# Transposing k before q for the first head pair of a top-k attention and squared-ReLU kernel, with new order tables

## The chip, the cores and the metric

The kernel runs on one NeuronCore of a Trainium2 chip. The core has five instruction streams: TensorE (PE: matrix products, transposes), VectorE (DVE), ScalarE (ACT), GpSimd (POOL) and SyncE (SP, which only issues DMAs). They run side by side and meet at semaphores. The metric is device time in microseconds (us) of one launch; lower is better.

## The reference

For 8 batches, 8 heads, 576 positions and a head width of 64, each row of scores keeps its 32 largest entries; the result of the attention feeds a two-layer network with a squared ReLU.

```python
def _attn_ref(q, k, v):
    scores = scale * np.matmul(q, k.transpose(0, 1, 3, 2))
    kth = np.partition(scores, -top_k, axis=-1)[..., -top_k:-top_k + 1]
    scores = np.where(scores >= kth, scores, -1000000000.0)
    attn = np.exp(scores - np.max(scores, axis=-1, keepdims=True))
    attn = attn / (np.sum(attn, axis=-1, keepdims=True) + 1e-09)
    return np.matmul(attn, v)

def _moe_ref(x, w_in, w_out):        # x: 4608 x 512, d_ff = 2048
    r = np.maximum(x @ w_in, 0.0)
    return (r * r) @ w_out
```

## The kernel before

**Units.** The heads are taken in pairs, 32 pairs in all. A unit is a block of 128 queries of one pair (or two 64-query ends of two pairs); there are 144, numbered here from 0. For each unit PE makes the scores of both heads into a slot of PSUM (the pool `large` has two slots), ACT copies them to the tile `s` (L1053), and DVE and POOL find the 32nd largest value of each row: DVE folds the score columns by maxima (L1131), lists the largest eight again and again (L1178, L1193, L1173) and ends with `kth` (L1196, once for each head); POOL does two integer passes between (L1126). ACT turns `s` and `kth` into the mask `w` (L1219, once for each head), PE transposes `s` and adds the mask to it in PSUM (the products `ident,s` and `steep_bf,w`), ACT takes the exponential `p` (L1285), PE multiplies by v, and so on. When all heads of a block of rows are done, PE runs the network on it (`xt,win`, then `wo,g`), with ReLU on ACT (L1443) and squares on POOL (L1458) or ACT.

**Order.** Every operation is declared with `pl.op(engine, ...)`: `r` names tiles that it reads (it then waits for all operations that write them), `hold` a tile that it merely occupies, `after` operations to wait for, `order` operations that it must only be issued behind. `arrange` doesn't schedule: the table `ORDER` lists for each engine the operations in the order in which they are issued, and `SLOT` lists the slot of each tile. In `ORDER["pe"]` small numbers are warm-up products of `ones_bf` by itself, 128x512, which write a PSUM bank that nothing reads, and a negative number is a spare: three products of `ident_bf` into an idle part of a score tile. Both only keep TensorE at work.

**The first pair.** `load_first` (L892) loads it by seven DMAs (L904): k's rows 0 to 511 of head 0 and the last 64 rows of both heads on ACT's queue, and on SP's queue k's rows 0 to 511 of head 1, q's first 128 rows of both heads (tile `rq`), and the rest of q (tile `rq2`). The two DMAs on ACT's queue are one operation with one semaphore, `d_rk0`; the one on SP's queue has `d_first`. `first_pair` (L917) then transposes on PE: `o_x` turns q's first 128 rows, `o_k` the four main blocks of k, and a third one the last 64 rows of k. `o_k` is bound behind `o_x` and reads `rk`, so it waits for all three loads of k. DVE copies k's main rows to the tile `qk` (L934), ACT the other two parts (L933, L935), and unit 0's scores can start. From the second pair on `load_pair` (L947) does the same in six DMAs on SP's queue (L955, L956), with the copies on ACT (L1006 to L1008).

**The end.** `verdict` (L1691) checks on DVE, from kept maxima, whether a fast way of finding the 32nd value was valid, and sets a flag; if it was not, the whole is done again by a slower way (which the profiled execution doesn't enter). Its operations (L1703 to L1733) stand among the last units' in DVE's order.

Of the kernel before, what the change touches and what calls it, by code (L numbers as in the profile page):

```python
# [663 lines left out]
def bass_top_k_attn__then__act_relu_squared_kernel(  # L664
# [219 lines left out]
    def build(full, weights, pl):  # L884
# [7 lines left out]
        def load_first(b, hp, rq, rq2, rk, base):  # L892
# [10 lines left out]
            def start(queue, *parts):  # L903
# [8 lines left out]
                  sem=slot_sem, ndma=1)  # L912
            pl.op("sp", 3.5, base - 79, start(
                nc.sync, lambda: part(rq2, q, 0, 1, 3), lambda: part(rq2, q, 1, 1, 3), lambda: rest(rq2, q, 512, 0)),
                w=[rq2], take=[rq2], sem=slot_sem, ndma=3)

        def first_pair(rq, rq2, rk, rv, qk, vb, base):  # L917
            tk, tx, tq = Tile(psum), Tile(psum), Tile(psum)
# [816 lines left out]
    main = Plan()  # L1735
# [108 lines left out]
```

## Time and profile before

| what | value |
|---|---|
| median of 3 runs | 745.13 us (744.3 to 746.08) |
| the profiled execution's own time | 746.16 us |
| its span, first to last instruction | 744.3 us |
| granted TensorE clock, mean | 0.995 of 2.4 GHz |
| busy: DVE, ACT, PE, POOL | 719.4, 717.3, 706.4, 685.9 us |
| PE products: warm-up of `ones_bf`, spares of `ident_bf` | 56, 138 |

The profiled execution's span is 1.86 us below its own time, and its own time is 1.03 us above the median. Four engines are busy for over 90% of the span, so what one engine loses is not made up elsewhere unless that engine has idle time later. "Busy" counts the stretch in which at least one instruction of the engine is under way. The row of an instruction says how long the engine was idle before it and which instruction ended the idle time.

### The profile page before, as it was taken

The numbers are of one execution on the slowest core, as the hardware profiler recorded it, in microseconds if no ns is written. First come the engines' busy times: TensorE is split into PE (matmuls) and PEld (weight loads), VectorE is DVE, ScalarE is ACT, GpSimd is POOL, SyncE is SP. The second block draws the span as 40 slices with busy tenths as digits, with TensorE's granted clock in tenths as the row PEclk, the third lists the DMA queues.
The fourth block names the chain that finished last, engine by engine and source line by source line (L and its number), as shares of the span: only waits on it lengthen the run. The fifth ranks groups of instructions, "written<-read, shape, count | busy, mean of one in ns | idle before, by whom it ended". The sixth has DMA issues, their size and how long they took to land.

```text
span 744.3 us, 27788 instructions
## 1 busy us (share of the span) xinstructions
PE 706.4 (95%) x10712; PEld 530.0 (71%) x10712; DVE 719.4 (97%) x3397; ACT 717.3 (96%) x1276; POOL 685.9 (92%) x529
## 2 busy tenths in 40 slices
PE   8898899999999999989999999999999999999997
PEld 4565777767677676767778677777777777777876
DVE  5999999999999999999999999999999999999996
ACT  4899999999999999999999999999999999999984
POOL 3799999999999999999999999999999999999971
PEclk9999999999999999999999999999999999999999
DMA  9766544254342432134311733121643115211101
GB/s 181 165 170 175 134 102 73 70 87 78 67 84 48 84 79 52 44 70 85 82 35 36 125 92 64 27 48 56 117 75 80 28 44 93 58 35 32 37 16 51
DMA packets 172730, 57.31 MB, mean 77 GB/s; under 512 B 157744, under 2 KB 164912, under 8 KB 172592
## 3 DMA queue, kind: packets, MB, share of 16 engines
q1 hardware_dynamic: 164528, 51.19, 30.2%
q0 software_dynamic: 7392, 4.13, 4.7%
q8 instruction: 85, 1.39, 0.8%
q14 instruction: 53, 0.43, 0.2%
q10 hardware_dynamic: 672, 0.16, 0.1%
HBM read 40.83 MB, written 13.57 MB: 73 GB/s over the span
## 4 chain that ended last, share of the span: by engine, by line
ACT 59%; PE 21%; DVE 16%; issue 3%; ACTq 0%
PE ps L875 17%; ACT w L1219 16%; ACT p L1285 12%; ACT s L1053 12%; ACT g L1443 6%; ACT s L1183 5%; DVE s L1131 4%; PE ps L878 4%; DVE s L1193 3%; DVE c L1178 3%; ACT av L1388 2%; DVE kth L1196 2%; DVE s L1173 2%; ACT o L1479 2%; ACT g L1461 1%
## 5 line engine op out<-in xcount | busy, mean ns | idle before, releaser
L1126 POOL TENSOR_TENSOR u<-s 128x864 int32<-128x864 int32 x142 | 244.7, 1723 | 22.1 <-DVE s L1131 20.8
L1219 ACT ACTIVATE w<-s,kth 128x576 bf16<-128x576 f32 x286 | 245.9, 918 | 2.9 <-DVE kth L1196 2.8
L1126 POOL TENSOR_TENSOR s<-s,u 128x864 int32<-128x864 int32 x142 | 243.1, 1714 | 3.2
L1178 DVE MAX8 c<-s 128x8 f32<-128x106 f32 (+2 forms) x864 | 203.3, 264 | 0.0
L1131 DVE TENSOR_TENSOR s<-ps,s 128x288 f32<-128x288 f32 x432 | 192.2, 445 | 9.9 <-ACT s L1053 7.7
L875 PE MATMUL ps<-qk 64*128 64x192 f32 (+3 forms) x1280 | 179.5, 430 | 8.5 <-DVE s L1131 4.6
L1053 ACT COPY s<-ps 128x1152 f32<-128x1152 f32 (+1 forms) x145 | 180.2, 1244 | 4.8 <-PE ps L875 4.1
L1285 ACT ACTIVATE p<-ps 128x1152 bf16<-128x1152 f32 x143 | 180.9, 1265 | 1.7 <-PE ps L875 1.5
L1193 DVE MATCH_REPLACE8 s<-c,s 128x92 f32<-128x92 f32 (+2 forms) x716 | 179.5, 254 | 0.0
L875 PEld LDWEIGHTS ps<-qk 64*128 64x128 f32 (+1 forms) x1280 | 130.8, 176 | 39.3 <-DVE s L1131 11.4
L875 PE MATMUL ps<-wo,g 128*128 128x512 bf16 (+1 forms) x592 | 144.5, 374 | 0.8 <-ACT qk L1007 0.4
L875 PE MATMUL ps<-xt,win 128*128 128x256 bf16 (+1 forms) x1280 | 130.7, 252 | 1.7 <-ACT g L1443 0.9
L1196 DVE MAX8 kth<-s 128x8 f32<-128x296 f32 x288 | 127.9, 454 | 0.3 <-POOL s L1186 0.2
L1173 DVE MAX8 s<-s 128x8 f32<-128x288 f32 x288 | 125.3, 446 | 0.3 <-POOL s L1126 0.2
L878 PEld LDWEIGHTS ps<-ident,s 64*128 64x128 f32 x2592 | 97.0, 139 | 35.9 <-ACT w L1219 13.5
L878 PE MATMUL ps<-ident,s 64*128 64x64 f32 x2592 | 112.4, 228 | 8.8 <-ACT w L1219 7.1
L875 PEld LDWEIGHTS ps<-xt,win 128*128 128x128 bf16 x1280 | 99.0, 98 | 21.0 <-issue 4.0
L1443 ACT ACTIVATE g<-ps 128x512 bf16<-128x512 f32 x140 | 98.2, 745 | 0.2
L1458 POOL TENSOR_TENSOR g<-g 128x1024 bf16<-128x1024 bf16 x50 | 94.6, 1892 | 3.8 <-ACT g L1443 3.7
L875 PEld LDWEIGHTS ps<-wo,g 128*128 128x128 bf16 x592 | 50.2, 98 | 48.1 <-issue 4.3
L1183 ACT ACTIVATE s<-s,c 128x140 f32<-128x140 f32 x148 | 76.4, 558 | 0.0
L875 PEld LDWEIGHTS ps<-vb,p 128*128 128x128 bf16 (+1 forms) x1600 | 54.6, 101 | 22.7 <-ACT p L1285 4.5
(92 smaller groups left out, 779.0 us busy)
## 6 DMA issues: line engine op xcount, KB each, us to landing
out_dram<-o SPq DMA_DIRECT2D x32, 256.0 KB, 2.8
rk<-in_k_dram SPq DMA_DIRECT2D x63, 128.0 KB, 2.6
rq<-in_q_dram SPq DMA_DIRECT2D x62, 128.0 KB, 2.6
s<-s SPq DMA_DIRECT2D x144, 32.0 KB, 1.9
g<-in_moe_w_in_dram SPq DMA_DIRECT2D x8, 512.0 KB, 4.4
g<-in_moe_w_out_dram SPq DMA_DIRECT2D x8, 512.0 KB, 4.1
vd<-in_v_dram POOLq DMA_DIRECT2D x14, 288.0 KB, 4.5
vb<-vd SPq DMA_DIRECT2D x56, 64.0 KB, 2.3
```

What stands on the lines that cost most here:

```text
L875: return pe.matmul(o, l, r, start=start, stop=stop, skip_group_check=True)
L878: return pe.matmul(o, i, ident, is_transpose=True, skip_group_check=True, **kw)
L1053: return pl.op("act", .14 + 2 * (c1 - c0) / 1200, pl.at("copy", tg - LEAD + 1), lambda: act.copy(at(st)[:, :, c0:c1], two(banks(ss)[:, FIR ...
L1126: return pl.op("gp", dur, prio, lambda: gp.tensor_tensor(o().bitcast(I32), x().bitcast(I32), y().bitcast(I32), op), **kw)
L1131: return dve(.36, lambda: vec.tensor_tensor(o(), two(banks(ss)[:, FIRST_AT + c:], SECOND, QUART), x(), ALU.max), r=[ss], **kw)
L1173: prev[i] = [dve(.0685 + HALF / 960, lambda i=i: vec.max(area(LIST, LIST + 8, i), area(LESS, LESS + HALF, i)), after=prev[i] + [low], hold ...
L1178: lambda i=i, t=t, span_=span_: vec.max(eighth(t, i), span_(i)),
L1193: lambda i=i, t=t, span_=span_: vec.match_replace(span_(i), eighth(t, i), span_(i), NEG), hold=[st])]
L1196: ks.append(chain(kth, i, prev[i], .0685 + (8 + HALF) / 960, lambda i=i: vec.max(eighth(kth, i), area(BIGS - QUART, LIST + 8, i)), hold=[st]))
L1219: masks[i:] = [pl.op("act", .77, pl.at("mask", tw + .8 * i), lambda i=i: act.activation(at(wt)[:, i, :], at(st)[:, i, 0:S], ACTF.Relu, bia ...
L1285: return act.activation(at(pt)[:, :, :].rearrange("p c (h q) -> p h c q", h=2), bass.AP(x.tensor, x.offset, [x.ap[0], [APART, 2], [64, 9], ...
L1443: return act.activation(at(g)[:, g0:g0 + 512], bank(hh)[:, 0:512], ACTF.Relu)
```

## The change

The four DMAs keep their queues and their order. The two on ACT's queue become two operations: the main rows (`main`, with the load on SP's queue), and the last 64 rows (`edge`) with a semaphore of their own. In `first_pair` the order of the transposes is turned: `o_k` comes first and waits for `main` alone, `o_x` follows, then k's last 64 rows, which wait for `edge`. The planned durations of these operations are new numbers; they only feed the bookkeeping of `arrange`. The tables `ORDER` and `SLOT` are new as a whole. By count, each engine issues the same instructions as before, except that PE has 49 warm-up products instead of 56 and 105 spares instead of 138. In the block ahead of the first transposes there are 6 warm-up products instead of 9, and ahead of the second pair's there are 2 instead of 5.

```diff
     "pe": (
-        "90 91 92 93 94 95 96 97 98 2541 2542 2543 2547 2574 2579 101 100 104 106 102 2613 2614 2615 2620 2648 -4979 -4979 -4979 -4979 -4979 126 119 129 134 "
+        "136 94 188 91 222 100 2542 2543 2544 2548 2575 2580 148 244 2614 2615 2616 -4979 -4979 -4979 2621 -4979 -4979 2649 2687 2689 2688 2694 2578 2757 "
...
-            pl.op("sp", .1, base - 82, start(nc.scalar, lambda: part(rk, k, 0, 0, 4),
-                                             lambda: rest(rk, k, 512, 0)),
-                  w=[rk], take=[rk], sem=slot_sem, ndma=2, via="act")
-            pl.op("sp", 4.0, base - 81, start(nc.sync, lambda: part(rk, k, 1, 0, 4)), w=[rk], sem=lambda o: "first", ndma=1)
-            pl.op("sp", 3.5, base - 80, start(nc.sync, lambda: (at(rq)[:, 0, :, :], both)), w=[rq], take=[rq],
+            main = [pl.op("sp", 3.3, base - 82, start(nc.scalar, lambda: part(rk, k, 0, 0, 4)),
+                          w=[rk], take=[rk], sem=slot_sem, ndma=1, via="act")]
+            edge = pl.op("sp", 4.2, base - 81.9, start(nc.scalar, lambda: rest(rk, k, 512, 0)), w=[rk], sem=lambda o: "edge",
+                         ndma=1, via="act")
+            main.append(pl.op("sp", 2.5, base - 81, start(nc.sync, lambda: part(rk, k, 1, 0, 4)), w=[rk],
+                              sem=lambda o: "first", ndma=1))
+            pl.op("sp", 2.65, base - 80, start(nc.sync, lambda: (at(rq)[:, 0, :, :], both)), w=[rq], take=[rq],
                   sem=slot_sem, ndma=1)
-            pl.op("sp", 3.5, base - 79, start(
+            pl.op("sp", 2.1, base - 79, start(
                 nc.sync, lambda: part(rq2, q, 0, 1, 3), lambda: part(rq2, q, 1, 1, 3), lambda: rest(rq2, q, 512, 0)),
                 w=[rq2], take=[rq2], sem=slot_sem, ndma=3)
+            return main, edge
...
-            o_x = pl.op("pe", .15, base - 45.2, flips(tx, rq, [0]), r=[rq], w=[tx], take=[tx, qk])
-            o_k = pl.op("pe", .5, base - 45.1, flips(tk, rk, [0, 1, 2, 3]), r=[rk], w=[tk], take=[tk], order=[o_x])
+            o_k = pl.op("pe", 1.03, base - 45.2, flips(tk, rk, [0, 1, 2, 3]), hold=[rk], w=[tk], take=[tk, qk], after=main)
+            o_x = pl.op("pe", .27, base - 45.1, flips(tx, rq, [0]), r=[rq], w=[tx], take=[tx], order=[o_k])
             pl.op("pe", .2, base - 45, lambda: tr(bank(tx)[:, 128:192], at(rk)[0:64, 4, :, :].rearrange("p h d -> p (h d)"),
-                                                  ident32[0:64, 0:64]), r=[rk], w=[tx], order=[o_k])
+                                                  ident32[0:64, 0:64]), hold=[rk], w=[tx], after=[edge], order=[o_x])
```

**PE from its start to the first scores.** Before (`ones_bf` is a warm-up product, `ident,rq` and `ident,rk` transposes of q and k, `qk` the scores; what stands behind "waits" are semaphores):

```order
L875 MATMUL ps<-ones_bf 128x512 [waits s_dve]
L875 MATMUL ps<-ones_bf 128x512
L875 MATMUL ps<-ones_bf 128x512 [waits s_pe] x7
L878 MATMUL ps<-ident,rq 128x128 [waits s_gp,d_rq0,s_pe]
L878 MATMUL ps<-ident,rk 128x128 [waits d_first,d_rk0]
L878 MATMUL ps<-ident,rk 128x128 x3
L878 MATMUL ps<-ident,rk 128x64
L875 MATMUL ps<-qk 128x192 [waits s_dve,s_act]
```

In the change (its line numbers are lower by one on PE, higher by two behind `load_first`):

```order
L874 MATMUL ps<-ones_bf 128x512 [waits s_dve]
L874 MATMUL ps<-ones_bf 128x512
L874 MATMUL ps<-ones_bf 128x512 [waits s_pe] x3
L874 MATMUL ps<-ones_bf 128x512
L877 MATMUL ps<-ident,rk 128x128 [waits d_first,d_rk0,s_gp,s_pe]
L877 MATMUL ps<-ident,rk 128x128 x3
L877 MATMUL ps<-ident,rq 128x128 [waits d_rq0,s_pe]
L877 MATMUL ps<-ident,rk 128x64 [waits d_edge]
L874 MATMUL ps<-qk 128x192 [waits s_dve,s_act]
```

Three warm-up products are gone, the four main transposes of k stand ahead of that of q, and k's last 64 rows wait for `d_edge`, which the main ones no longer wait for.

**PE at unit 4's scores (the third pair's first unit) and unit 0's masked transposes (`ident,s`, `steep_bf,w`).** Before:

```order
L878 MATMUL ps<-ident,rk 128x128 [waits s_pe]
L878 MATMUL ps<-ident,rk 128x128 x3
L875 MATMUL ps<-ident_bf 128x128 [waits s_act]
L875 MATMUL ps<-ident_bf 128x128 x2
L878 MATMUL ps<-ident,s 128x64 [waits s_act]
L878 MATMUL ps<-ident,s 128x64 x16
L878 MATMUL ps<-ident,s 128x64 [waits fence]
L875 MATMUL ps<-steep_bf,w 128x64 x17
L875 MATMUL ps<-steep_bf,w 128x64 [waits fence]
L875 MATMUL ps<-qk 128x192 [waits s_act,s_dve]
L875 MATMUL ps<-qk 128x384 x2
L875 MATMUL ps<-qk 128x192 [waits fence]
```

In the change:

```order
L877 MATMUL ps<-ident,rk 128x128 [waits s_act]
L877 MATMUL ps<-ident,rk 128x128 x3
L874 MATMUL ps<-qk 128x192 [waits s_dve,s_act]
L874 MATMUL ps<-qk 128x384 x2
L874 MATMUL ps<-qk 128x192 [waits fence]
L877 MATMUL ps<-ident,s 128x64 [waits s_dve,s_act]
L877 MATMUL ps<-ident,s 128x64 x16
L877 MATMUL ps<-ident,s 128x64 [waits fence]
L874 MATMUL ps<-steep_bf,w 128x64 x17
L874 MATMUL ps<-steep_bf,w 128x64 [waits fence]
```

The scores of unit 4 stand ahead of unit 0's masked transposes, not behind them, and the three spares between are gone.

**DVE at the last unit (L1212 and L1214 write the last unit's mask, L1703 and L1705 are operations of `verdict`).** Before:

```order
L1193 MATCH_REPLACE s<-c,s 128x2x70 [waits s_dve]
L1178 MAX c<-s 128x8 [waits s_dve]
L1196 MAX kth<-s 128x8 [waits s_dve]
L1193 MATCH_REPLACE s<-c,s 128x2x70 [waits s_dve]
L1196 MAX kth<-s 128x8 [waits s_dve]
L1703 TENSOR_TENSOR signs<-signs,c 128x2x67
L1212 TENSOR_SCALAR w<-s,kth 128x512 [waits d_d3,s_pe,s_dve]
L1395 RECIPROCAL rzall<-av 128x4 [waits s_act]
```

In the change:

```order
L1180 MAX c<-s 128x8 [waits s_dve]
L1195 MATCH_REPLACE s<-c,s 128x2x70 [waits s_dve]
L1397 RECIPROCAL rzall<-av 128x4 [waits s_act]
L1198 MAX kth<-s 128x8 [waits s_dve]
L1214 TENSOR_SCALAR w<-s,kth 128x512 [waits s_dve]
L1705 TENSOR_TENSOR c<-c 128x2x67
L1397 RECIPROCAL rzall<-av 128x2 [waits s_act]
L1705 TENSOR_TENSOR c<-c 128x2x67
```

The `verdict` operation that stood ahead of the last mask now comes behind it. The same holds for the one over `c`, which before stood 46 rows further up and is here the row behind the mask.

## Rows read from the trace of the kernel before

**Rows 1.** Busy time by stages: stretch, us, busy PE, PEld, DVE, ACT, POOL (instructions), clock, DMA.

```profile
0.00:30.00 30.00, 24.77 (x186) 14.95 (x188) 20.45 (x89) 16.56 (x24) 14.18 (x43) 0.94 0.89 177
30.00:627.00 597.00, 569.54 (x8652) 427.20 (x8644) 589.97 (x2801) 595.92 (x1065) 576.53 (x417) 1.00 0.37 79
627.00:741.00 114.00, 112.09 (x1890) 87.90 (x1888) 108.86 (x511) 104.84 (x189) 95.24 (x70) 1.00 0.17 38
```

**Rows 2.** Timeline, 0 to 9 us: start, duration, engine, instruction, idle before.

```profile
0.75 0.47 SPq L904 DMA_DIRECT2D rk<-in_k_dram  x1
0.76 1.25 ACTq L904 DMA_DIRECT2D rk<-in_k_dram  x2
...
1.07 4.02 PE L875 MATMUL ps<-ones_bf 128*128 128x512 bf16 x9 [1.07 <-DVE ones_bf L1622]
1.28 2.34 SPq L904 DMA_DIRECT2D rq<-in_q_dram  x4
...
5.15 0.47 PE L878 MATMUL ps<-ident,rq 128*128 128x128 f32 x1
...
5.42 1.16 PE L878 MATMUL ps<-ident,rk 128*128 128x128 f32 x5
...
6.42 0.69 DVE L934 COPY qk<-ps 128x512 f32<-128x512 f32 x1 [5.40 <-PE ps L878]
...
7.25 1.24 PE L875 MATMUL ps<-qk 64*128 64x192 f32 x8 [0.67 <-DVE qk L934]
...
8.96 1.44 DVE L1131 TENSOR_TENSOR s<-ps,s 128x288 f32<-128x288 f32 x3 [1.85 <-ACT s L1053]
```

**Rows 3.** Line L904, issues of 0.7 to 1.0 us: issue to landing.

```profile
DMA to landing us min/median/max: 3.0/3.2/3.3
```

**Rows 4.** Line L904, all seven issues: issue to landing.

```profile
DMA to landing us min/median/max: 2.9/3.1/3.5
```

**Rows 5.** Timeline of PE, 5 to 9 us: the last product of the first nine.

```profile
4.46 0.63 PE L875 MATMUL ps<-ones_bf 128*128 128x512 bf16 x1
```

**Rows 6.** Tile rk, 0 to 12 us: weight loads, ns least, median, most.

```profile
L878 PEld LDWEIGHTS ps<-ident,rk x5: 134/230/231, 5.2 to 6.3; 128*128 128x128 f32 x4, 64*128 64x128 f32 x1
```

**Rows 7.** Tile rq, 0 to 12 us: the same.

```profile
L878 PEld LDWEIGHTS ps<-ident,rq x5: 137/142/181, 5.2 to 8.9; 128*128 128x128 f32 x4, 64*128 64x128 f32 x1
```

**Rows 8.** Timeline of ACT, 13 to 40 us.

```profile
14.42 0.27 ACT L1008 COPY qk<-ps 128x128 f32<-128x128 f32 x1
...
21.23 1.44 ACT L1219 ACTIVATE w<-s,kth 128x576 bf16<-128x576 f32 x2 [1.04 <-DVE kth L1196]
...
24.16 1.13 ACT L1285 ACTIVATE p<-ps 128x1152 bf16<-128x1152 f32 x1 [1.02 <-PE ps L875]
26.25 1.12 ACT L1053 COPY s<-ps 128x1152 f32<-128x1152 f32 x1 [0.96 <-PE ps L875]
...
31.68 1.14 ACT L1053 COPY s<-ps 128x1152 f32<-128x1152 f32 x1
```

**Rows 9.** Timeline of PE, 12 to 26 us.

```profile
13.28 0.63 PE L878 MATMUL ps<-ident,rk 128*128 128x128 f32 x4 [0.30 <-DMA rk<-in_k_dram]
...
22.73 0.91 PE L878 MATMUL ps<-ident,s 64*128 64x64 f32 x18 [1.50 <-ACT w L1219]
...
23.93 2.27 PE L875 MATMUL ps<-qk 64*128 64x192 f32 x8
```

**Rows 10.** Busy time by stages, 20 to 30 us, columns as in Rows 1.

```profile
23.00:26.50 3.50, 3.50 (x45) 2.73 (x40) 3.50 (x17) 1.52 (x3) 3.02 (x5) 0.53 0.88 254
```

**Rows 11.** Timeline of DVE, from 27 us and from 712 us.

```profile
27.40 0.46 DVE L1131 TENSOR_TENSOR s<-ps,s 128x288 f32<-128x288 f32 x1 [0.81 <-ACT s L1053]
...
712.59 1.69 DVE L1703 TENSOR_TENSOR c<-c 128x134 f32<-128x134 f32 x1
...
726.14 1.39 DVE L1703 TENSOR_TENSOR signs<-signs,c 128x134 f32<-128x134 f32 x1
```

**Rows 12.** Timeline of PE, 712 to 745 us.

```profile
719.29 0.27 PE L878 MATMUL ps<-ident_bf,x 128*128 128x128 bf16 x2 [0.38 <-POOL x L1397]
```

More of the change, by code (lines that the diff above doesn't have):

```diff
@@ L32 @@
     "pe": (
[43 rows of a table removed]
-    "act": (
[38 rows of a table removed]
-    "dve": (
[121 rows of a table removed]
[42 rows of a table added]
+    "act": (
[38 rows of a table added]
+    "dve": (
[121 rows of a table added]
 }
 SLOT = (
-    "01010101010101010010101010010100000000000000001000000000000001010000000000001000000000000000000000000000000000000000000000000000000000000100"
-    "00000000000000000000000000001000100000000000000000000000000001110100001000000001010000000000000000000000000000000000000000000000000000000000"
+    "01010101010101010111110100000101010000000000001000000000000000100000000000000000000000000000000000000000000000100001000000100000000100000000"
+    "00000000010001000000000000011001100000000001100000000000000001110100001000000000100000000000000000000000000000000000000000000000000000000000"
     "00000000000000000000000000000000000000000000000000000000000000000000000000000000000000000000000000000000000000000000000000000000000000000000"
@@ L267 @@
-    "110016121001100010100111110001200111110011010030100100400010010512000006010100000101110000000011110100001201010010130012020001213011")
+    "00000000000000000000000000000000000000000000000000000000000000000000000000000000000010100000001011001000010110102000213000010011102012040101"
+    "15001010001030031610001001011010011102013000111100120002000013111111400000511010000160012110011101100011121112030010100010111201300000104141"
+    "00400000511010000010001602020000100001051110111101120010110011201131102040000100001100200310011151110100600011000101010102121210000030011111"
@@ new lines @@
+    "41100050001116020200100010001011021030101114015000102031101001012111110013041113021214100010110410011501010600100001011110001001100110000101"
+    "10210310011120110010300101411010050002161000100000011010011211120000113111204001010000111021031001110102000501001610110001503110002120110001"
+    "00102140002011113000001013001104010205000010000110021031100116111110000000111111012000213110000104000111151010060101010001211011000001011021"
+    "03010011410511010011001200110300100001402111411120500001001011311060111001000110150410010010020011100001101200310011131010100401011502000061"
@@ new lines @@
+    "01200010010101100101102011113001010401021500100010101102113000011021011010010006111000103120101403000000111014100010011210120011000310000401"
+    "01100050010060101110002001100110110011102013010011210021300101004000015101110006010210001001010000120101100011101201301001101040001210111300"
+    "10000000100115120004011110015100001060111010100000001111010010011010020000110301001001400010005010001001011001610001110000110111010010121001"
+    "00101011101301001114001011015111000160011000201000000313101141410100000000010001112010111001000111121000211100003001010004110000150011100001"
@@ L270 @@
+    "101006121011000000100011110100200110100111000130100000400011011512000006011110110011110000010111110100001201010010030012020101203011")
 class Pool:
@@ L906, in load_first, with first_pair @@
             both = bass.AP(q.tensor, q[b, 2 * hp, 0:P, :].offset, [[D, P], [S * D, 2], [1, D]])
-            pl.op("sp", .1, base - 82, start(nc.scalar, lambda: part(rk, k, 0, 0, 4),
-                                             lambda: rest(rk, k, 512, 0)),
-                  w=[rk], take=[rk], sem=slot_sem, ndma=2, via="act")
-            pl.op("sp", 4.0, base - 81, start(nc.sync, lambda: part(rk, k, 1, 0, 4)), w=[rk], sem=lambda o: "first", ndma=1)
-            pl.op("sp", 3.5, base - 80, start(nc.sync, lambda: (at(rq)[:, 0, :, :], both)), w=[rq], take=[rq],
+            main = [pl.op("sp", 3.3, base - 82, start(nc.scalar, lambda: part(rk, k, 0, 0, 4)),
[5 more added lines that the diff above has]
+            pl.op("sp", 2.65, base - 80, start(nc.sync, lambda: (at(rq)[:, 0, :, :], both)), w=[rq], take=[rq],
                   sem=slot_sem, ndma=1)
-            pl.op("sp", 3.5, base - 79, start(
+            pl.op("sp", 2.1, base - 79, start(
                 nc.sync, lambda: part(rq2, q, 0, 1, 3), lambda: part(rq2, q, 1, 1, 3), lambda: rest(rq2, q, 512, 0)),
                 w=[rq2], take=[rq2], sem=slot_sem, ndma=3)
-        def first_pair(rq, rq2, rk, rv, qk, vb, base):
+            return main, edge
+        def first_pair(rq, rq2, rk, rv, qk, vb, base, main, edge):
             tk, tx, tq = Tile(psum), Tile(psum), Tile(psum)
@@ L972, in load_pair @@
                 rq2 = tile("rq")
-                load_first(b, hp, rq, rq2, rk, base)
+                main, edge = load_first(b, hp, rq, rq2, rk, base)
             else:
@@ L985, in load_pair @@
             if via:
-                return first_pair(rq, rq2, rk, rv, qk, vb, base)
+                return first_pair(rq, rq2, rk, rv, qk, vb, base, main, edge)
             tq, tk, tx = Tile(psum), Tile(psum), Tile(psum)
```

11 lines of the change are left out of this document (removed), and 397 rows, old and new, of the table ORDER.

## Prediction

> **What bounds the kernel now.** I read the busy time by stages first. Over the first 30 us no engine but PE is busy for even 70% of the time; from 30 to 627 us ACT works for 595.92 of 597 us and DVE for 589.97; from 627 to 741 us PE works for 112.09 of 114 [rows 1]. So there are three stages: a start in which engines wait for each other, a long stage that ACT fills, and an end that PE fills. In the second stage only 1.08 us of idle time of the filling engine is left, in the third 1.91. Since each engine issues the same work as before (but for warm-up products and spares), a gain must come from the start, or out of these 3.0 us.
>
> The timeline of the start shows a chain without slack: warm-up products, six transposes, two kinds of copies, unit 0's scores at 7.25, ACT's copy, DVE's first fold at 8.96 [rows 2]. The transposes begin at 5.15, right behind the last warm-up product, which starts at 4.46 and takes 0.63 [rows 2, 5]. The DMAs had landed by then: the two main loads of k are issued at 0.75 and 0.76 and land 3.0 to 3.3 us later, so at 3.75 to 4.06 [rows 2, 3]. The last 64 rows of k are issued at about 1.3 (ACT's two issues take until 2.01) and q at 1.28; with the longest landing of all seven, 3.5, both are there by 4.8 [rows 2, 4]. What holds the first transpose is the warm-up, not a load.
>
> **The change, part by part.** *Three warm-up products fewer ahead of the transposes.* The nine start from 1.07 to 4.46, that is 0.424 apart [rows 2, 5]; the sixth starts at 3.19 and ends at 3.82. Then k's main rows are the last to come, at 4.06 at the latest. I put the first transpose at 4.1, against 5.15: 1.05 earlier.
>
> *k first, with a semaphore for its last rows.* The six transposes are the same; they took from 5.15 to 5.42 + 1.16 = 6.58, so 1.43, and unit 0's scores followed 0.67 later [rows 2]. In the new order q's turn comes some 1.2 us after 4.1 and the last rows' turn behind it, both past 4.8, so neither new wait ends later than its turn, and nothing queued behind them on PE waits longer. Had the old wait for all of k stayed, the start would have been 4.8 at the latest, so this edit is worth up to 0.7 of the 1.05 and the products the rest. Transposes end at 5.53, scores start at 6.2, the first fold at 7.9 (8.96 less 1.05). DVE's copy L934 begins 1.1 earlier too, and ends ahead of ACT's copies, which still release the scores.
>
> *Three products fewer ahead of pair 2's transposes.* Nothing: PE waits there for pair 2's k, which lands at 13.28 [rows 9]. SP issues the same DMAs in the same order over the whole start, so this landing doesn't move. Nor do unit 2's scores get earlier: ACT now copies k's last rows ahead of its main ones, which by the duration of the copies (0.27 and 0.58, the first begun at 14.2) puts them at 15.1, some 0.3 later than now. Cover: DVE has units 0 and 1 to list, and after 11.35 it has no wait of over 0.3 us until 27.40 [rows 11]. By the new order 31 of its instructions stand ahead of unit 2's first fold, some 11 us of work from 7.9 on, and the scores' copy would be there at 17.5. Without that cover the head start would be lost.
>
> *Unit 4's scores ahead of unit 0's masked transposes.* Now PE waits 1.50 for the mask, runs the masked transposes, and then makes unit 4's scores at a granted clock of 0.53 of full (mostly the level of 1.2 GHz), in 2.27 instead of 1.24 [rows 2, 9, 10]; ACT waits 0.96 for them and DVE 0.81 [rows 8, 11]. In the new order these scores wait for the third pair's copies on ACT alone: by the durations at about 22.6, copied by 25.0, or 26.0 at the half clock. DVE, with the same instructions ahead of it as now, gets there at 27.40 - 0.81 - 1.05 = 25.5, so its 0.81 goes, or shrinks to 0.5. But ACT, which fills the next stage, decides: laying out its operations by hand until it has done the same set that ends at 32.8 now [rows 8], I end at about 31.7. It loses its waits of 1.04, 1.02 and 0.96 [rows 8] only to find others of 0.6 to 0.7, for the masks come no earlier than DVE gives them. So I carry 1.05 on, and DVE's 0.8 is slack.
>
> *The rest of the tables.* From 30 to 627 us nothing in the trace before prices an unknown order. Bounds: a gain of 1.08 (all of ACT's idle time), a loss of some waits like those of the start, each near 1.0. I take 0, since ACT is full already.
>
> *The end.* Two operations of the verdict, 1.69 and 1.39 on DVE, stand ahead of the last units' lists and of the last mask [rows 11], and move behind it. But PE, which fills this stage, waits only 0.38 in one place, for POOL, itself waiting for DVE [rows 12]; what is late next is PE's own queue. Bounds: 0 and the stage's 1.91; I take 0.4, nearest to the one wait that shows.
>
> *Spares.* 33 spares and the other warm-up products less: they run where PE waits anyway, so nothing, unless the clock falls (below).
>
> Sum: -1.05 - 0.4 = -1.45. The profiled execution took 746.16, its span 744.3 and 1.86 around it, and would take 744.7. It is 1.03 above the median of the runs shown, 745.13; from the median the same sum gives **743.7**.
>
> **The rivals.** *The new order closes more gaps.* ACT's 1.08 and PE's other 1.5 are there to be had, and DVE arrives early with 0.8 of slack. Against: these gaps are many and small. All of it: 741.1; a typical share of half: 742.4.
>
> *The head start is spent.* Either at unit 2, if DVE runs out of units 0 and 1 (for: pair 2's landing is fixed), or at the clock. The weight loads of the first 128-wide transposes of k take 230 ns, later ones of q 142; the load of k's last rows, at 6.3, takes 134, as the same shape does later [rows 6, 7]. So PE ran slowly until about 6.1, although the granted clock reads full there, and unit 0's scores at 6.2 would just miss that. The new order has less work ahead of them, and a pause of 0.3 us. If the faster rate comes late, unit 0's scores take 2.27 instead of 1.24 and the 1.05 is gone: 745.13 - 0.4 = 744.7; with unit 1's too it is 745.1 or more. The Trainium skill (TensorE: Matmul & The Clock Gate, What's actually happening) says that the throttled state is the default and that activity releases it, which speaks against taking work away here. By that rule the fast rate comes later the less PE does; the trace agrees as to the slow start (230 against 142 ns), and shows no case with less work.
>
> *Slower: the clock falls more often.* With 40 products fewer, and PE waiting for masks in the first 110 us, more stretches like that of 23 to 26.5 us could come. That one cost ACT its waits of 1.02 and 0.96, 1.98 together. One more stretch makes 745.7, two make 747.6; from two on the change is slower. For: waits of PE of 1.5 us like that at 22.73 [rows 9]. Against: at unit 4 the new order puts scores into such a wait, not spares.
>
> *The change doesn't do what it says:* k's main rows land only when PE would have started anyway. They'd have to take 4.3 us instead of 3.3, and seven loads show at most 3.5 [rows 4]. Then 744.7.
>
> **How the numbers follow.** A measurement of this kernel can tell about 0.2%, 1.5 us, from no change: faster means below 743.64, slower above 746.6. The forecast, head start plus a little of the end, gets 0.45; its own range is 742.7 to 744.6, half of it below the mark (0.22 faster, 0.23 same). More gaps closed: 0.22, faster. Head start spent: 0.20, same. Clock falls: 0.10, slower. Doesn't do it: 0.03, same. That is 0.44 faster, 0.46 same, 0.10 slower. The range runs from 741.7, which leaves out the far end of the first rival, to 745.6, which leaves out the falling clock: at most 0.15 outside.
>
> **What would show it.** Right: the first `ident,rk` product at 4.1 (3.9 to 4.3), unit 0's scores at 6.2 and still 1.24 long, the first fold at 7.9, pair 2's k still landing near 13.3, no wait of DVE near 27 us, ACT full from about 29 us on. For the second rival: scores of over 1.3 us before 10 us, or a fold of unit 2 that waits. For the slower one: further stretches of granted clock near 0.5 with waits on ACT beside them. Wrong altogether: a first transpose later than 4.8, or a head start at 30 us that is gone at 627.

## Result and profile after

The changed kernel takes 749.42 us (median of 8 runs, 748.13 to 753.04) against 745.56 for the kernel before (8 runs): a ratio of 1.0055, 95% interval 1.0042 to 1.0069. It is slower by 0.55%, where 743.7 was forecast with a range up to 745.6. The profiled execution took 748.13, its span 746.3; it is the shortest of the eight, so its profile shows only about half of the loss.

The busy time by stages of the changed kernel, columns as in [rows 1]:

```profile
0.00:30.00 30.00, 21.15 (x141) 14.23 (x141) 21.02 (x91) 15.56 (x24) 14.48 (x42) 0.94 0.76 167
30.00:627.00 597.00, 566.12 (x8575) 424.27 (x8625) 587.21 (x2786) 595.43 (x1064) 575.61 (x419) 1.00 0.37 80
627.00:743.00 116.00, 109.89 (x1897) 88.55 (x1906) 109.19 (x522) 106.42 (x191) 96.29 (x70) 1.00 0.15 37
```

Against [rows 1] ACT has done 1.0 less by 30 us, and no stage looks broken (the last one is cut 2 us later, since the span ends 2 us later). So I looked for places, not for a stage. The start first, to set beside [rows 2] (timeline: start, duration, engine, instruction, idle before):

```profile
1.07 3.46 PE L874 MATMUL ps<-ones_bf 128*128 128x512 bf16 x6 [1.07 <-DVE ones_bf L1624]
...
2.17 0.10 PEld L874 LDWEIGHTS ps<-ones_bf 128*128 128x128 bf16 x1 [0.96 <-PE ps L874]
2.83 0.10 PEld L874 LDWEIGHTS ps<-ones_bf 128*128 128x128 bf16 x1 [0.56 <-PE ps L874]
3.50 0.13 PEld L874 LDWEIGHTS ps<-ones_bf 128*128 128x128 bf16 x2 [0.56 <-PE ps L874]
...
4.33 1.06 PE L877 MATMUL ps<-ident,rk 128*128 128x128 f32 x4
...
6.37 2.29 PE L874 MATMUL ps<-qk 64*128 64x192 f32 x8 [0.47 <-ACT qk L935]
...
9.14 1.44 DVE L1133 TENSOR_TENSOR s<-ps,s 128x288 f32<-128x288 f32 x3 [3.02 <-ACT s L1055]
```

The transposes are early as forecast, but unit 0's scores take 2.29 instead of 1.24, and the first fold comes 0.18 later than before. By the new PSUM places four of the six products follow each other in one place; each waits for the one ahead, and they start 0.67 to 0.69 apart, not 0.42.

Then the stretch from 160 to 180 us, of the kernel before and of the changed one (same columns as above):

```profile
160.00:180.00 20.00, 19.86 (x291) 15.14 (x289) 19.76 (x95) 20.00 (x37) 19.39 (x16) 1.00 0.49 101
```

```profile
160.00:180.00 20.00, 18.47 (x272) 13.83 (x269) 18.90 (x90) 18.88 (x34) 18.77 (x17) 1.00 0.71 127
```

ACT, full before, loses 1.12 here, and the DMA engines are busy for 0.71 instead of 0.49. The timelines tell why; first the kernel before, then the changed one:

```profile
150.09 1.04 POOL L1397 TENSOR_TENSOR x<-av,rzall 128x512 bf16<-128x512 f32 x1
151.16 1.24 SPq L1412 DMA_TRANSPOSE xt<-x  x1
159.86 0.70 ACT L1479 COPY o<-ps 128x512 f32<-128x512 f32 x1
162.44 0.59 SPq L1487 DMA_DIRECT2D out_dram<-o  x1
```

```profile
154.10 1.05 POOL L1399 TENSOR_TENSOR x<-av,rzall 128x512 bf16<-128x512 f32 x1
155.18 1.24 SPq L1414 DMA_TRANSPOSE xt<-x  x1
158.26 0.69 ACT L1481 COPY o<-ps 128x512 f32<-128x512 f32 x1
162.50 0.68 POOL L1674 DMA_DIRECT2D vd<-in_v_dram  x1
...
164.86 0.66 POOL L1674 DMA_DIRECT2D vd<-in_v_dram  x1
...
166.06 0.59 SPq L1489 DMA_DIRECT2D out_dram<-o  x1
...
170.58 0.59 ACT L1481 COPY o<-ps 128x512 f32<-128x512 f32 x1 [1.12 <-DMA out_dram<-o]
```

POOL computes one `x` 4 us later, behind a `g` and a `u`; SP's transposes wait for it, and with them all that SP issues behind. The output that ACT had ready at 158.95 leaves at 166.06 and takes 4.44 to land (2.30 before), while two loads of `vd` (288 KB each) run that stood 35 us apart before (167.36 and 202.69). ACT's next copy into that `o` waits 1.12.

Last the end. PE's last product of the work proper ends at 740.31, before at 740.23. The verdict's product, of the kernel before and of the changed one:

```profile
740.79 0.20 PE L1731 MATMUL ps<-fone 128*1 128x12 f32 x2 [0.56 <-DVE fone L1729]
```

```profile
741.78 0.20 PE L1733 MATMUL ps<-fone 128*1 128x12 f32 x2 [1.48 <-DVE fone L1729]
```

And the code fetches from 741 to 747 us (queue, packets, MB, share of the DMA engines), before and after:

```profile
q14 instruction: 4, 0.03, 2.0%
```

```profile
q14 instruction: 5, 0.04, 2.6%
```

Beside the fifth stands a longer branch behind the flag, by the trace's records: on DVE 2.56 us pass from its compare-and-branch (743.49) to its next instruction (746.05), 0.64 in the kernel before. The other engines take 0.5 to 0.6 in both. Before, POOL's closing drain (1.28 long) ended last and covered DVE; now DVE ends 1.25 behind POOL's. The last of the five fetches starts only at 746.6, so DVE did not wait for that one; in every profile of this case one fetch starts 0.56 to 0.70 behind DVE's next instruction. The extra one is among the four ahead of it, and the trace doesn't say for which engine. DVE's stream has 3524 records instead of 3554; the 30 that are gone are waits on semaphores, which the new order needs no more. (The count ahead of the prediction, by which the engines issue the same instructions, leaves such waits out: the other streams have 1 to 22 more of them.)

So of the 2.0 us between these two spans 1.9 lie behind the last product of the work proper: 0.92 up to the verdict's product and 0.98 behind it. In this pair of profiles what ACT lost near 170 us had been made up by then.

### The profile page after: what moved, and what is told of

Its sections match the earlier page's. It is cut to its first block, busy times and chain, and to the rows that moved or that the text cites. A ratio compares the mean times of both kernels' runs of the same rounds, so it can differ in the third digit from the quotient of the medians.

```text
span 746.3 us, 27655 instructions
## 1 busy us (share of the span) xinstructions
PE 697.2 (93%) x10607; PEld 527.1 (71%) x10672; DVE 717.4 (96%) x3397; ACT 717.4 (96%) x1276; POOL 686.4 (92%) x529
## 3 DMA queue, kind: packets, MB, share of 16 engines
q0 software_dynamic: 7392, 4.13, 4.8%
## 4 chain that ended last, share of the span: by engine, by line
ACT 68%; PE 11%; DVE 10%; POOL 5%; issue 5%; DMA 1%; ACTq 0%; SPq 0%; POOLq 0%
ACT w L1221 19%; ACT p L1287 14%; ACT s L1055 13%; PE ps L874 9%; ACT s L1185 6%; ACT g L1445 6%; DVE s L1133 3%; ACT av L1390 2%; DVE s L1195 2%; PE ps L877 2%; POOL u L1128 2%; ACT g L1463 2%; DVE c L1180 2%; ACT o L1481 2%; ACT qk L1009 2%
## 5 line engine op out<-in xcount | busy, mean ns | idle before, releaser
L1180 DVE MAX8 c<-s 128x8 f32<-128x92 f32 (+2 forms) x864 | 204.9, 265 | 0.1
L1055 ACT COPY s<-ps 128x1152 f32<-128x1152 f32 (+1 forms) x145 | 182.7, 1266 | 6.3 <-PE ps L874 6.0
L1287 ACT ACTIVATE p<-ps 128x1152 bf16<-128x1152 f32 x143 | 183.9, 1286 | 0.4 <-PE ps L874 0.3
L1195 DVE MATCH_REPLACE8 s<-c,s 128x106 f32<-128x106 f32 (+2 forms) x716 | 180.1, 256 | 0.0
L874 PE MATMUL ps<-wo,g 128*128 128x512 bf16 (+1 forms) x527 | 130.2, 373 | 10.0 <-issue 5.2
L874 PE MATMUL ps<-xt,win 128*128 128x256 bf16 (+1 forms) x1280 | 132.3, 252 | 1.1 <-ACT qk L1010 0.3
L874 PEld LDWEIGHTS ps<-xt,win 128*128 128x128 bf16 x1280 | 97.4, 98 | 22.2 <-issue 3.5
L1445 ACT ACTIVATE g<-ps 128x512 bf16<-128x512 f32 x140 | 100.0, 753 | 0.0
L1185 ACT ACTIVATE s<-s,c 128x140 f32<-128x140 f32 x148 | 80.2, 587 | 0.0
```

Of the source, the lines that this page charges most:

```text
L874: return pe.matmul(o, l, r, start=start, stop=stop, skip_group_check=True)
L1055: return pl.op("act", .14 + 2 * (c1 - c0) / 1200, pl.at("copy", tg - LEAD + 1), lambda: act.copy(at(st)[:, :, c0:c1], two(banks(ss)[:, FIR ...
L1180: lambda i=i, t=t, span_=span_: vec.max(eighth(t, i), span_(i)),
L1195: lambda i=i, t=t, span_=span_: vec.match_replace(span_(i), eighth(t, i), span_(i), NEG), hold=[st])]
L1287: return act.activation(at(pt)[:, :, :].rearrange("p c (h q) -> p h c q", h=2), bass.AP(x.tensor, x.offset, [x.ap[0], [APART, 2], [64, 9], ...
L1445: return act.activation(at(g)[:, g0:g0 + 512], bank(hh)[:, 0:512], ACTF.Relu)
```

## Experiments

Every time is a median beside the kernel before on the same chip, then the recorded ratio with its 95% interval. That ratio isn't exactly the quotient of the two medians; the two differ by up to 0.0011 here. The theories A to G are named in the expectations.

**Start and later orders apart.** The changed kernel, its six products in turns between two PSUM places (three entries of `SLOT`, written out here by product):

```diff
 PSUM places of products 136 94 188 91 222 100
-0 1 1 1 1 0
+1 0 1 0 1 0
```

> The changed kernel, and only the PSUM places of its first six warm-up products differ: they take turns between two places, as the nine of the kernel before do. In the changed kernel four of the six follow each other in one place, each waits for the end of the one ahead, and they start 0.67 us apart instead of 0.42. Theory A (what PE does in the first 4 us decides when the clock rises): the products end near 3.6, the first transpose starts at 3.8 to 4.1, the clock is at its upper level from about 6.1 us on (9.63 in the changed kernel), unit 0's scores take 1.24 instead of 2.29, the first fold starts at 7.9, and the time is 1.0 to 1.6 below the changed kernel's 749.4, so 747.8 to 748.4. Theory B (six products are too few, however they stand): the clock still rises past 9 us, the scores take 2.2 or more, and the time stays at 749.4. Theory C (the later orders alone carry the loss): the start improves as in A, and the time stays above 748.8.

749.88, 1.0049 (1.0031 to 1.0067). The start improved as in A (clock at its upper level from 3.98 on, scores 1.24, first fold 7.48), the time did not: theory C. (The first transposes came at 4.26, hardly earlier than the changed kernel's 4.33: k's main rows landed at 4.13 here.) This profiled run, 753.02, also shows what makes some runs so long. ACT waited 2.9 for the output, PE behind it, and then the clock fell:

```profile
174.00:182.00 8.00, 6.76 (x32) 4.94 (x32) 6.78 (x32) 6.43 (x13) 5.39 (x4) 0.57 0.35 71
```

The kernel before with the new start alone, products in turns (the first lines of the tables; the numbers behind are shifted by one):

```diff
 "pe":
-90 91 92 93 94 95 96 97 98 2541 2542 2543 2547
+90 91 92 93 94 95 2542 2543 2544 2548
 "sp":
-2535 2536
+2535 2536 2537
```

> The kernel before, with the change's start alone: k's main rows waited for by themselves and transposed ahead of q, and six warm-up products instead of nine, in turns between two places; every later order as in the kernel before. If the later orders carry the loss (theory C), the time is at or below the kernel before: 744.5 with the whole head start of 1.05, 745.6 with none of it. If the start carries it (six products make the clock rise late, theory B), unit 0's scores take over 2 us, the first fold comes at 9 or later, and the time is 746 to 748.

746.73, 1.0012 (1.0001 to 1.0023). In the profiled run, 745.60, the first fold came at 7.83 and the verdict's product at 740.23, 0.56 ahead of the kernel before; but five of twelve runs took 747.3 to 747.6. Neither forecast fits: the start is as early as theory C has it, and the median is theory B's. The head start alone made nothing faster.

The old start with the new later orders (tables joined at 13 us; one line shown):

```diff
 "pe":
-136 94 188 91 222 100 2542 2543 2544 2548
+90 91 92 93 94 95 96 97 98 2541 2542 2543 2547
```

> The kernel before up to unit 1's scores and pair 2's first transposes (nine warm-up products, q transposed first, one wait for all of k), with the change's later orders and PSUM places. The clock should rise at 6.1 us as in the kernel before. If the later orders carry the loss (theory C): 748 to 749.5. If the start carries it (theories A and B): 745 to 746.

749.21, 1.0047 (1.0032 to 1.0061): the later orders carry the loss, with the old start as with the new one. DVE's branch took 3.73.

The kernel before without products 96, 97 and 98:

```diff
-95 96 97 98 2541
+95 2541
```

> The kernel before without the last three of its first nine warm-up products, nothing else. The transposes then start when all of k and q have landed, at 4.5 to 4.8 instead of 5.15. Theory A (six products that stand close are enough): the clock rises at 6.1 to 6.6, unit 0's scores take up to 1.5, the time is 744.9 to 745.6. Theory B (six are too few): the clock rises past 9 us, unit 0's scores take over 2 us, the first fold comes at 9.0 to 9.5, and the time is 745.6 to 747.

746.69, 1.0009 (0.9998 to 1.0019). The clock rose only at 15.6, unit 0's and unit 1's scores took 2.29 each, the first fold came at 9.42. That fits B, though e1 and e2, with as many products, rose at 4 to 5; see the last section.

**The branch at the end.** 60 met waits, two to an instruction, in the changed kernel:

```diff
                 ins.then_inc(self.sems[e], 1)
+            if o.idx == ("dve", 1):
+                for _ in range(60):
+                    eng.wait_ge(self.sems["dve"], 1)
```

> The changed kernel with 30 more instructions on DVE, semaphore waits that are met already, right behind its first operation, where DVE is idle until about 5 us. The changed kernel's DVE stream is 30 instructions shorter than that of the kernel before (3524 against 3554 records, all 30 of them waits), and in it DVE's branch at the end takes long: from DVE's compare-and-branch to its next instruction 2.56 us (3.48 and 3.73 in the other two kernels with the new later orders), against 0.64 in the kernel before and in both kernels with the old later orders. Theory D (what counts is where the branch lies in DVE's code): with 3554 records again it takes 0.64, there is a code fetch near 736 us, and the time falls by 1.9 to 3.1, to 746.3 to 747.5. Theory E (the branch is slow because of what happens near it, the late verdict or another engine's fetches): it stays at 2.5 to 3.7 and the time at 749.4.

The branch takes 0.64. The fifth late fetch is gone, and one at 726.5 is there instead (727.7 in the kernel before; the changed one has none on this queue between 713.4 and 743.9):

```profile
q14 instruction: 4, 0.03, 2.0%
```

The fetch stands earlier than I expected, and the branch is as theory D has it. The time isn't: 748.61 (six runs, 745.70 to 751.31), 1.0060 (1.0042 to 1.0077), no lower than the changed kernel's. Three of the six runs had a lower mean granted clock (0.992 against 0.995 to 0.997); hence the same kernel again in the square below.

The same in the kernel before, with `range(196)`:

> The kernel before with 98 more met waits on DVE at the same place, nothing else: 3652 records, which is the changed kernel's 3524 and 128 more, a whole number of the 8192-byte pieces in which this code is fetched if an instruction takes 64 bytes. Theory D: DVE's branch at the end takes 2.5 to 3.7 instead of 0.64, and the kernel before becomes 1.9 to 3.1 slower, 747.4 to 748.6, with no other change in the trace. Theory E: 745.5, the branch at 0.64.

753.39, 1.0119 (1.0104 to 1.0133). The branch took 3.30, with five late fetches (window 746 to 753): theory D holds for the branch, in the old orders too. The rest of the time is a fault of my experiment: these instructions took 0.1 us each, not nothing, so DVE's first copy came at 11.09, the start lost 4.7, and the clock was at its lower level from 10.0 to 20.3.

```profile
q14 instruction: 5, 0.04, 1.9%
```

**The late output and the verdict.** With the 30 waits, POOL's `x`:

```diff
 "gp":
-3620 3200 3649 3365 3606
+3620 3365 3200 3649 3606
```

> The kernel with 30 more waits, and on POOL one operation moved: the `x` of the chunk whose transposes SP issues at 155.2 us stands ahead of the product `g` and of one `u`, as in the kernel before, instead of behind both. In the changed kernel it ends at 155.1 instead of 151.1; SP, whose transposes wait for it, issues everything behind them some 4 us later, the output of `o` that ACT copied at 158.3 at 166.1 instead of 162.4, while two loads of `vd` of 288 KB move; ACT's next copy into that `o` at 170.6 waits 1.1 for it (2.2 and 2.9 in two other kernels with these orders). Theory F (that chain costs what is lost between 160 and 180 us): SP issues that output at 162.0 to 163.0, ACT waits for no output near 170, the 1.1 to 1.8 that the engines fall back between 160 and 200 us are gone, and the time is 1.0 to 1.8 below the kernel with 30 waits alone. Rival: the 1.8 come from another wait there (PE for ACT, DVE for POOL), and the time stays.

745.98, 1.0020 (1.0007 to 1.0032), SP's issue at 162.75, ACT's wait 0.6: 2.6 below the kernel with the waits alone, more than F's 1.0 to 1.8; I put the excess down to the scatter of the other one's runs, which isn't shown.

The reverse, in the kernel before:

```diff
 "gp":
-3619 3364 3648 3605 3199
+3619 3199 3648 3364 3605
```

> The kernel before, and on POOL only that one `x` stands behind one product `g` and one `u`, as in the change; all else as before. If that place is what delays the output: SP issues it at 165 to 167 instead of 162.4, ACT waits 0.5 to 2 for it near 170, and the time is 0.5 to 2.6 above the kernel before, with a wider spread of runs if PE's wait lets the clock fall. If the loss needs the other moved orders too: within 0.3 of the kernel before.

745.48, 0.9998 (0.9988 to 1.0008). The output left as late as expected, and nobody waited:

```profile
159.85 0.70 ACT L1479 COPY o<-ps 128x512 f32<-128x512 f32 x1
...
165.02 0.59 SPq L1487 DMA_DIRECT2D out_dram<-o  x1
```

So the late `x` alone isn't the cause; here no load of `vd` stands ahead of the output, the next is issued at 167.90. Two tries on the verdict, first two operations with the 30 waits alone, then nine with `x` ahead as well:

```diff
 "dve":
-8253 8173 8251 8211 8212 8258 8259 8214 8262 8252
+8253 8251 8252 8173 8211 8212 8258 8259 8214 8262
```

> The kernel with 30 more waits, and on DVE two operations of the verdict (`c` at 729.96 and `signs` of 134 columns at 733.49) moved ahead of the reciprocal at 729.87, into DVE's idle time of 1.67 before it. In the changed kernel the verdict's last product on PE comes at 741.78 instead of 740.79, 1.47 behind the last product of the work proper. If the verdict's list ends the kernel: that product comes 0.4 to 0.8 earlier, and the time is as much below that of the kernel with 30 waits alone. If the list waits for the last `g` and `fone` anyway, it moves by less than 0.2.

748.28, 1.0056 (1.0042 to 1.0069); the lag stayed at 1.49, since the list behind the last `g` was as long as before.

```diff
 "dve":
-8253 8173 8251 8211 8212 8258 8259 8214
+8253 8251 8252 8255 8256 8265 8173 8267 8211 8212 8258 8259 8268 8214 8279 8280
```

> The kernel with 30 more waits and POOL's `x` ahead, and now nine operations of the verdict's list on DVE stand earlier: five fill DVE's idle time before the reciprocal at 729.9, one that before the next reciprocal at 731.0, one that before the copy of `xt` at 733.3, and the two reductions of `rzall`, which need nothing later, follow that copy. In every kernel with the new later orders the verdict's product on PE comes 1.48 behind the last product of the work proper, in those with the old ones 0.55. The move of two operations alone left it at 1.49, since the list behind the last `g` stayed as long. If the length of that list behind the last `g` is what ends the kernel: the lag falls to 0.5 to 0.7, and the time lies 0.8 to 1.0 below the kernel without this move (745.98 beside a kernel before of 744.94), so about 0.1 above the kernel before. If something else ends it, the lag stays at 1.4 to 1.5.

745.86, 1.0000 (0.9986 to 1.0013); the lag fell to 0.91, not 0.55. What the lag costs isn't shown: against e7's 1.0020 the intervals overlap.

**Repairs of the start.** Products 96 to 98 moved behind unit 1's scores, in the second experiment's kernel:

```diff
 "pe":
-2580 101 100 104 106 102 2614
+2580 101 100 104 106 102 96 97 98 2614
```

> The kernel before with the change's start, as the second experiment, but the three warm-up products that the start gives up are moved, not dropped: they stand behind unit 1's scores, where PE waited 1.25 us for pair 2's q. In the second experiment the profiled run was 0.56 faster than that of the kernel before, but the median was 1.2 slower, with runs of 747.4 to 747.6 at a lower granted clock (0.992 to 0.994), and its clock fell at 15.2 us, after that wait. If the clock's falls are what the start costs, and PE's empty stretch brings them: no fall before 20 us, median 744.4 to 745.0. If the falls come anyway: 746 to 747 as before.

745.45, 0.9999 (0.9987 to 1.0012). That lies between my two forecasts. The clock didn't fall in the profiled run, 744.19, 1.3 below the median; three of twelve runs still took over 747, one of them (747.52) at a mean granted clock of 1.0, so the clock alone doesn't make runs long.

All repairs (e1's places, three more products in front of 2614, and e5, e7, e9):

> All repairs on the changed kernel: six products that take turns between two PSUM places, three more products ahead of pair 2's transposes, 30 more waits on DVE, POOL's `x` ahead, the verdict's list earlier. If the four causes (start 0.5 to 1, branch 1.9 to 3.1, the wait for the output 1.1 to 2.6, the verdict 0.9) are the whole loss: 743.5 to 745.0, at or below the kernel before. If the later orders cost something else as well: 746 or more.

745.32, 0.9999 (0.9986 to 1.0012). The loss is undone, though the time is 0.3 above the range that I expected.

**A square on one chip: waits, and `x` ahead.** No edit beyond those of e5 and e7.

> The changed kernel once more, as the corner without either repair of a square of four on one chip: 30 waits on DVE or not, POOL's `x` ahead or not. 749.0 to 750.0; DVE's branch at the end 2.5 to 3.7; ACT's wait for the output near 170 us 1 to 3.

> The changed kernel with POOL's `x` ahead, without the 30 waits. If branch and output cost independently: the branch still takes 2.5 to 3.7, no wait of over 0.7 for the output, and the time lies 1.5 to 2.6 below the changed kernel and 1.9 to 3.1 above the one with both repairs. If the 30 waits bring nothing to the time (their kernel stood at 1.0060 of the kernel before, the changed one at 1.0055): as fast as with both, 746.

> The changed kernel with the 30 waits alone, again. If the branch's 1.9 to 3.1 show in the time: 746.5 to 747.5, and the earlier median of 748.61, of six runs between 745.7 and 751.3, was high because the clock fell in several of them. If they don't: as the changed kernel, within 0.5.

> Both repairs together, again: 745.5 to 746.5, and 3.0 to 4.5 below the changed kernel.

| | `x` late | `x` ahead |
|---|---|---|
| 30 waits less | 749.69, 1.0056 (1.0041 to 1.0070) | 748.66, 1.0044 (1.0031 to 1.0057) |
| 30 waits back | 746.87, 1.0031 (1.0020 to 1.0042) | 745.90, 1.0010 (1.0001 to 1.0019) |

The branch shows in the time: 2.8 in either column by the medians, 1.9 and 2.5 by the ratios, and it took 3.22 and 3.15 in the upper row, 0.64 in the lower. POOL's order brings 1.0 in either row by the medians, 0.9 and 1.6 by the ratios, less than I expected; in the upper row the intervals overlap. No sign shows that one effect depends on the other, but the intervals are about 1 us wide to either side. The weak corner is that of the waits alone, 1.0060 on the earlier chip and 1.0031 here. With `x` ahead the branch's price doesn't hang on it: 1.0044 without the waits, 1.0010 and 1.0020 with them.

In the profile of both together ACT still waited for an output that left as early as before:

```profile
162.17 0.59 SPq L1492 DMA_DIRECT2D out_dram<-o  x1
...
169.50 0.59 ACT L1484 COPY o<-ps 128x512 f32<-128x512 f32 x1 [1.30 <-DMA out_dram<-o]
```

**The load of `vd` apart.** On top of both:

```diff
 "gp":
-3712 69 3504
+3712 3504
-4050 4051
+4050 69 4051
```

> The kernel with both repairs, and one of POOL's loads of `vd` moved back to where the kernel before has it. In the changed kernel two such loads of 288 KB start at 162.5 and 164.9, in the kernel before one at 167.4 and the other some 40 us later. With both repairs SP issued the output at 162.2, as early as in the kernel before, and ACT still waited 1.3 for it near 170. Theory G (the two loads in a row make the output late, not only SP's place): the output lands within 4 us, ACT's wait for it is gone in the profile, and the time falls by 0.5 to 1.0 below 745.9. Rival: the wait stays, or goes without a change of the time, as the engines have other waits there.

744.42, 0.9983 (0.9968 to 0.9999), a larger gain than theory G's. ACT's wait is gone, the stretch is full again, and the DMA share is back at 0.50; first with both repairs, then with the load apart too:

```profile
160.00:180.00 20.00, 18.37 (x247) 13.40 (x247) 19.07 (x92) 18.70 (x33) 19.11 (x17) 1.00 0.81 117
```

```profile
160.00:180.00 20.00, 19.93 (x287) 14.72 (x284) 19.81 (x96) 20.00 (x37) 19.62 (x16) 1.00 0.50 99
```

All 20 profiles together say what makes this output late, and it isn't the pair of loads as such. Issued ahead of the loads, it lands 2.3 to 2.6 us later (ten profiles, two of them with both loads right behind it); issued behind the first of them or both, 4.4 to 7.3 (ten profiles). Moving the load took away the one ahead.

All repairs and the load:

> All repairs: the start with products in turns and three more ahead of pair 2's transposes, 30 waits, POOL's `x` ahead, the verdict's list earlier, and now the load of `vd` apart. If the causes add: 744.3 to 745.0, at or a little below the kernel before (the four without the load stood at 0.9999 of it). If the load brings nothing: 745.3.

744.84, 0.9983 (0.9969 to 0.9997). So places of the products and the verdict's list add nothing that can be measured. The version with waits, `x` and load alone beats the kernel before by 0.17%, just clear of the noise.

## Why the prediction was wrong

**The step that failed** is "The rest of the tables ... I take 0", and with it the sum, which had no term for the end of the program. I bounded the unknown order by a loss of "some waits ... each near 1.0" and then took none of it into the range.

- *Moves on POOL that I never walked through.* I looked at SP's order for the start alone. It is the same in both tables, and still SP's issues move later on: SP waits for POOL's `x` before it goes on, POOL's list puts it behind a `g` and a `u`, and a load of `vd` now stands ahead of the output. Moving `x` is worth about 1.0 (square), the load 1.9 (745.90 at 1.0010, then 744.42 at 0.9983). The place shows: from 150 to 200 us ACT works for all of the 50 us in the eight profiles with the loads apart, and for 44.9 to 49.7 in the twelve with the loads together; from 200 to 627 us it works for 426.8 to 426.9 in all twenty. The rival of a falling clock was near: in e1's profile the clock fell in PE's wait there. I had placed it in the first 110 us and given it 0.10.
- *The branch.* Not among the terms: I counted work, and no waits. It costs 1.9 to 2.8 by the square; the profiles show 1.25 to 2.44 (DVE's end behind POOL's drain, in five profiles). The two agree within the noise.
- *The end.* "-0.4" had the wrong sign in the profile: DVE waited 1.67 and 1.46 behind the mask for ACT and PE, and the moved operations lengthened the list behind the last `g`, so the verdict lags 1.48 instead of 0.56. What that costs in the median isn't shown.

**The main term failed too, in the step "So I carry 1.05 on".** The head start doesn't show in the time: the new start alone gave 1.0012 (three products dropped) and 0.9999 (moved), and with the new orders the old start (1.0047) does as well as the new one (1.0049 to 1.0056). I had ACT lose its waits near 20 us and find others of 0.6 to 0.7. In the changed kernel's profile these are 1.77 and 1.71, for the mask and for unit 4's scores, which came at the lower clock after all (2.29):

```profile
19.47 0.77 ACT L1221 ACTIVATE w<-s,kth 128x576 bf16<-128x576 f32 x1 [1.77 <-DVE kth L1198]
...
25.73 1.12 ACT L1055 COPY s<-ps 128x1152 f32<-128x1152 f32 x1 [1.71 <-PE ps L874]
```

What ACT has done by 35 us measures the lead. The kernel before, the one with the load apart (unit 0's scores 1.24) and the changed one (2.29), columns as in [rows 1]:

```profile
0.00:35.00 35.00, 28.45 (x254) 17.66 (x256) 25.45 (x112) 21.56 (x35) 18.55 (x46) 0.95 0.88 179
```

```profile
0.00:35.00 35.00, 25.05 (x226) 16.83 (x228) 26.84 (x121) 21.84 (x35) 18.34 (x45) 0.95 0.74 167
```

```profile
0.00:35.00 35.00, 25.18 (x193) 16.91 (x194) 25.66 (x114) 20.52 (x32) 17.99 (x44) 0.95 0.71 161
```

So of 1.05 some 0.3 is left at 35 us in the six profiles with this start where unit 0's scores take 1.24, and 1.0 to 3.8 is lost in the four where they take 2.29.

**What held.** The transposes at 4.1: they start at 4.17 to 4.33. In this profile k's main rows had landed by 3.73 and the products held them; with products in turns the transposes still start at 4.04 to 4.31, because k's main rows land at 3.91 to 4.13 there ("4.06 at the latest" was close). Pair 2's k at 13.28: 13.43. No wait of DVE near 27 us: none of over 0.3 from 11.6 to 32.6. The scores "at 6.2 and still 1.24 long" came at 6.37 and 2.29 in this run, as the second rival said. Of ten profiles of kernels with this start six show 1.24, with the first fold at 8.07 to 8.12, and four 2.29, with 9.13 or 9.14. Three profiles with the old start have it at 8.56, 8.79 and 8.96. So DVE's first fold is 0.4 to 0.9 earlier in some runs, and the clock takes that in others.

With the 30 waits back and two moves on POOL undone, the change stands at 0.9983 of the kernel before, 1.3 us faster (1.0 by the medians). That my sum of -1.45 is close to it is luck as far as the runs show: its main term, the start, brings nothing that can be measured by itself, and which part of the new orders brings the 1.3 stays open.

## What to carry to other kernels

A head start counts only as far as the engine that fills the next stage gets it. A table of new orders has to be read on every engine that another waits for: an unchanged queue moves when what it waits for moves, and a buffer's next writer pays at its end. Look for an output that comes to be issued behind a load, and whose buffer is soon needed. Where a program ends in a branch, compare each engine's time from the branch to the next instruction before costing anything else: a few instructions more or less in the stream moved it by 2 to 3 us.

## What the runs showed of the hardware

**A branch whose price hangs on its place in the code.** DVE's branch took 0.64 in all 14 profiles with 3554 records on DVE, and 2.56 to 3.73 in the six with 3524 or with 3652, which is 3524 and 128. In the changed kernel this queue's last fetch of 8192 bytes ahead of the branch is at 713.4, in the kernel before at 727.7, and five come behind the branch instead of four. The Trainium skill (Runtime: NRT & Kernel Launch, Instruction fetch mechanics) says that a taken branch whose target isn't among the two pages at hand forces a fetch before the engine goes on. That one fetch more comes with the stall, and that the price hangs on the place in the code, agrees with that; which fetch DVE waited for the trace doesn't tell. The pieces on this queue are 8192 bytes here, where the page has 16 KiB (only those of q8 are as large). Why the same jump takes 0.64 with 30 instructions more no run shows.

**When the clock first rises differs from run to run.** The trace's first record of the granted clock at 2.4 GHz is at 3.9, 4.0, 5.0, 5.3 and 5.6 us in the five profiles with the new start and products in turns, and anywhere from 5.5 to 14.1 in the ten with products that wait; with the old start it is at 5.3, 5.8 and 6.1, with six products and q first at 15.6. Durations agree: unit 0's scores take 2.29 ahead of it and 1.24 behind. Products in turns made it early in five of five, but a single profile of each kernel can't tell their order from chance. The Trainium skill (TensorE: Matmul & The Clock Gate, What's actually happening), by which activity releases the throttled state, would have the sparse start rise later; four of ten against none of five leans that way and no more.

**An output behind a load lands late.** Over the 20 profiles 521 outputs of 256 KB with no load of `vd` (288 KB, issued by POOL) around them landed 2.3 us after their issue in the median (2.0 to 4.6), and 84 issued while one such load was on its way 4.2 (2.5 to 5.9). Why, no run shows.

**A semaphore wait isn't free on DVE:** 98 instructions of two met waits each took some 10 us, 0.1 each.
